# Spectral swap with real and imaginary rows on even and odd partitions; two more slices transposed by DMA

## Chip, core and metric

The kernel runs on one core of a Trainium2 chip. The core has TensorE (PE), VectorE (DVE), ScalarE (ACT), GpSimd (POOL) and SyncE (SP), each with an instruction queue of its own, and 16 DMA engines. The metric is the device time of one execution in microseconds (us); a comparison rests on the median of several executions.

## What is computed

Two kinds of layers alternate, twice each, on a sequence of 2048 positions with 512 channels (bf16):

```
def A(q, k, v, shift_k, ssm_k, ssm_D):            # long convolution
    k_shift = sum over t of k_pad[:, t:t+S] * shift_k[:, 3-t]     # 4 taps
    kv = k_shift * v
    y = irfft(rfft(kv padded to 4096) * rfft(ssm_k padded to 4096))[:S]
    return q * (y + kv * ssm_D)

def B(x, w1, b1, w2, b2):                          # MLP, 512 -> 1376 -> 512
    return gelu(layernorm(x) @ w1 + b1) @ w2 + b2

x = A_q
x = x + A(layernorm(x), ...) ; x = x + B(layernorm(x), ...)
x = x + A(layernorm(x), ...) ; x = x + B(layernorm(x), ...)
```

The part y of A depends on k, v and the filter only, so it is computed once and used in both layers.

## The kernel before

**The front: the convolution.** The Fourier transform over time is split into two stages, both matmuls against tables. The filter `ssm_k` is transposed (tag `ht`), goes through stage 1 (`h1`, L764) and stage 2 (`h2`, L777) and becomes the spectrum H, in the region `R_H`. The table S2 of stage 2 has the real part in output rows 0 to 63 and the imaginary part in rows 64 to 127. For each frequency the complex product of H with the spectrum X of kv needs H once as it is and once with real and imaginary rows exchanged. The exchanged copy lies in `R_HS`; 16 DMAs of 256 KB each make it, from partitions 0 to 63 to 64 to 127 and back:

```
for kh in range(2):
    for d0, n in PARTS:
        for c in range(0, 128 * n, 4096):
            for g in range(2):
                src, dst = [A(64 * p, 64, r + o, [512, 8], [1, 256]) for p, r in ((g, R_H), (1 - g, R_HS))]
                dma(dst, src, 1 << 18, reads=[src], rate=210.0)
```

kv is made from k and v, for two groups of 128 channels by banded matmuls on TensorE (`shift_pe`, L808, L825, product with v L832) and for the other two by VectorE (`shift_tt`, the 128x2048 forms of L656). It goes through stage 1 (`x1`, L764) and stage 2 (`products`, tags `x2_0` and `x2_64` for the two parts of 64 groups of four channels, L870). Each PSUM result is copied to SBUF by ScalarE or VectorE (`evac`, L661 or L662), and VectorE multiplies it in place with H and the exchanged copy (L656). `inverse1` (`i1_0`, `i1_64`, L894, table U) and `inverse2` (`i2_0`, `i2_64`, L951, table T2) bring y back to the time domain.

**The rest: the layers.** Sixteen slices of 128 positions are taken in blocks: `BLOCKS0` = 1, 1, 2, 2, ... in the first pair of layers, four blocks of four slices in the second. For each slice VectorE makes statistics (L983, L985), GpSimd the inverse root (L989, L991), VectorE normalizes (L998), multiplies by y and adds (L656); statistics and normalization follow again for the MLP. The normalized slice is transposed into `R_XT`: slices 0 to 3 of the first pair of layers by four TensorE transposes (L1045) and a copy out of PSUM, all others by one DMA transpose issued on SP (L1037). `m1` (L1058) multiplies by w1, ScalarE applies the gelu (L1063), `m2` (L1091) multiplies by w2, and VectorE adds the result to x (L1095). The last slice has a finer form (L1080, L1084).

**The order.** Every operation is declared to a planner (`Prog`) with an assumed duration. `Prog._cells` maps operands to cells (in four groups of 32 partitions), from which the dependencies come. `schedule` then fixes the order on each engine and, for operations that either ScalarE or VectorE can do, the engine. It uses assumed durations and tables of biases by tag (`BIAS`, `SHY`) and by operation number (`PB`, `PS`, `HOLD`, `ENG`). Each engine works through its list in order. On SP the order is: inputs, table S2, U, W1, the swaps, T2, the x input `A_q`, W2, then the DMA transposes and the stores.

Of the kernel before, what the change touches and what calls it, by code (L numbers as in the profile page):

```python
# [44 lines left out]
class Prog:  # L45
# [6 lines left out]
    BIAS = {'': -521155, 'fir0': 1051798, 'fir1': 843097, 'fir2': 989049, 'fir3': 987651, 'h1': 1081037, 'h2': -15927, 'ht': 1112634, 'i1_0': 1897872, 'i1_64':  # L52
        1957624, 'i2_0': 1184460, 'i2_64': 1481308, 'm1': 2555275, 'm2': -1895730, 'q0': 888240, 'q1': 774644, 'q19': 368770, 'q2': 596884, 'q20':
        169092, 'q21': -27345, 'q22': 917115, 'q3': 746810, 'q4': 810080, 'q5': 973212, 'q6': 1402410, 'q7': 321282, 'q8': 747916, 'taps': 871203,
        'warm0': 1001221367, 'x1_0': 904949, 'x1_1': 332081, 'x1_2': 669567, 'x1_3': 179302, 'x2_0': 377722, 'x2_64': 1746588, 'y0': 402006, 'y1':
        377011, 'y19': 351016, 'y2': 526293, 'y20': 1353266, 'y21': 1084298, 'y22': 962110, 'y3': 501697, 'y4': 829124, 'y5': 1453849, 'y6': 1171227,
        'y7': 417695, 'y8': 201523, 'z0': 1335006, 'z1': 1302874, 'z19': 54792, 'z2': 645169, 'z20': 1225188, 'z21': 742421, 'z22': -322863, 'z3':
        -681085, 'z4': 290073, 'z5': -723046, 'z6': 31881, 'z7': 125204, 'z8': 150269}
    SHY = {'fir0': 1381, 'fir1': 0, 'h1': 616, 'h2': 0, 'ht': 1476, 'i1_0': 1122, 'i1_64': 0, 'i2_0': 355, 'i2_64': 600, 'x1_0': 0, 'x1_1': 0, 'x1_2': 0,
        'x1_3': 0, 'x2_0': 175, 'x2_64': 0, 'z0': 1278, 'z1': 0, 'z2': 218}  # L60
    PB = {0: 34576, 2: -79378, 3: 43127, 4: 998812279, 9: 1394230, 44: 1395437, 45: 1613596, 47: 734111, 49: 928776, 51: 998512784, 52: 998468674, 53: -251398,
        54: -275617, 55: -73100, 56: -94401, 57: -104470, 58: -97344, 59: -11254, 60: -108406, 61: -94351, 63: -1000973, 64: -999971, 65: 27771, 66:
        -77522, 67: -999603, 68: 141227, 69: -1000923, 70: -1052691, 71: 34934, 72: -77472, 73: 998216537, 74: 133836, 75: -847532, 76: -193783, 77:
        998086816, 78: 213997, 79: -845232, 80: -158480, 81: 998714645, 82: -29228, 83: 998096074, 85: -912875, 86: 81387, 87: -823698, 88: -168262,
        89: 998118247, 90: 94211, 91: 998328931, 92: 27535, 93: -765996, 94: -165174, 95: -789736, 96: -295, 97: -846123, 99: -845182, 100: -158430,
        101: 998114703, 102: -218608, 103: 998118297, 104: -163885, 105: 998086766, 106: 912895, 107: -54439, 108: 950031, 109: -33246, 110: 1149468,
        111: -31803, 112: 1348311, 113: 217100, 114: 974687, 115: 999587069, 116: 918924, 117: 999198541, 118: 903029, 119: 999587119, 120: 909361,
        121: 217391, 122: 694743, 123: 999618935, 124: 958333, 125: 999612320, 126: 1042905, 127: 219847, 128: 900863, 129: 999657213, 130: 964412,
        131: 999608609, 132: 768388, 133: 999620187, 134: 856071, 135: 999410698, 136: 724031, 137: 999546617, 155: 23799, 156: -162015, 157: -60642,
        158: -461494, 159: -153347, 161: -694106, 162: 1454, 163: -947997, 164: 207759, 165: 998395730, 166: -173754, 167: 998555574, 169: 998332526,  # L70
        170: -423295, 171: 998606664, 172: 38904, 173: 998455595, 175: 999072054, 176: 243913, 177: 154045, 178: 391385, 179: 999289091, 180: 348447,
        181: 999128447, 183: 29584, 184: -999103, 185: 998165866, 186: 998199123, 187: 998019345, 188: 998017691, 189: 998151553, 191: -646236, 192:
        -539651, 193: 998734714, 194: -523620, 195: 998581986, 196: -137633, 197: 998715658, 199: 86734, 200: 998494190, 201: 21973, 202: -495859,
        203: 47162, 204: 48952, 205: 59976, 207: 999452991, 208: -1197, 209: 878201, 210: 929976, 211: 999077641, 212: 730704, 213: 999240348, 215:
        999293389, 216: 725624, 217: 510366, 218: 999271422, 219: 646616, 220: 381726, 221: 999070258, 222: 94055, 223: 349589, 224: 999293339, 225:
        71120, 226: -10853, 227: 772848, 228: 711543, 229: 2558, 230: 999128706, 231: 107444, 232: -203830, 233: 1276613, 234: 384777, 235: -85060,
        236: 790445, 237: 75982, 239: -823960, 240: -697909, 241: 997632090, 242: -339336, 243: -1075953, 244: -656610, 245: -826734, 246: 50, 247:
        -1076003, 248: -339386, 249: 997632040, 250: -210520, 251: -489040, 252: -675432, 253: -825900, 255: -927034, 256: -854615, 257: -1353528,
        258: 997762488, 259: -607871, 260: -1334318, 261: -871126, 262: 997876284, 263: -1321, 264: -704597, 265: 997906582, 266: 148883, 267:
        -675809, 268: -909457, 269: -70780, 270: -56569, 271: -864218, 272: -104560, 273: -36737, 274: -577323, 275: -1480713, 276: -833598, 277:  # L80
        997878740, 279: -1162936, 280: 27, 281: -687297, 282: -121406, 283: -1363624, 284: -118911, 285: 997939634, 286: 577508, 287: -393821, 288:
        475975, 289: -885280, 290: -270112, 291: 997939684, 292: 576726, 293: 998145513, 308: 1177488, 309: 1198831, 310: 1304423, 311: 1244639, 312:
        971190, 314: 285666, 315: -57020, 316: 391644, 317: -46141, 318: 998762253, 319: -155518, 320: 135422, 321: -64658, 322: 346129, 324:
        998409091, 325: -1207668, 326: 998414402, 327: -319349, 328: -1037091, 329: -441577, 330: -1032463, 331: -1024485, 332: -884533, 334: -54361,
        335: -51188, 336: -3436, 337: 322745, 339: -19921, 340: 770364, 341: 119508, 343: 150496, 344: -815052, 345: -1074024, 346: -1087676, 347:
        -942418, 348: -900262, 349: -695458, 350: 351759, 351: -892088, 352: 1076614, 353: -2671, 354: 885814, 355: -1190402, 356: 1001895, 357:
        -1433063, 358: 1027075, 359: -1429074, 360: 1029921, 361: -1731382, 362: 919746, 363: -910238, 364: 41149, 365: -890772, 366: 1184682, 367:
        -897821, 368: -1245948, 369: -144705, 370: -1245720, 371: -401600, 372: 2730439, 373: 4887400, 374: 3740474, 375: 2124032, 377: 112340, 378:
        10032, 379: -338853, 380: -245578, 382: 104508, 383: 805647, 384: -77071, 386: -911065, 387: -70724, 388: -451068, 389: -405580, 390: -950972,
        391: -206569, 392: 187780, 393: 885471, 394: -1662575, 395: 1009734, 396: -1295021, 397: 1024703, 398: -1183431, 399: 1037432, 400: -1248538,  # L90
        401: -255605, 402: -654317, 403: -359159, 405: -1278286, 407: 1092663, 408: -888363, 409: 917474, 410: 814, 411: 890156, 412: -211373, 413:
        -358377, 414: 32750, 415: 5020518, 416: 4338250, 417: 3211311, 418: 2415420, 420: -46159, 421: -2327, 422: -267214, 423: 164122, 424: 265989,
        425: -113051, 427: 110610, 428: 892080, 429: 111401, 430: -44629, 431: -261436, 432: -173254, 433: -363932, 434: 23598, 436: 42311, 437:
        12952, 438: -285134, 439: -300486, 440: 216702, 441: 228190, 442: 255444, 443: 205358, 444: 625548, 445: -22042, 446: 108479, 447: 664113,
        448: 1243693, 449: 863420, 450: -179909, 451: -322256, 452: -471129, 453: 1004937, 454: -629654, 455: 863470, 456: -761928, 457: 1009668, 458:
        -890636, 459: -156707, 460: -292462, 461: -1267645, 462: -913360, 463: -782357, 464: -540612, 465: -252368, 466: -913588, 467: -1302020, 468:
        -435191, 469: -251282, 470: -907822, 471: 3209413, 472: 3720996, 473: 4860599, 474: 3269555, 475: 3378084, 476: 4978144, 477: 4979058, 478:
        2905911, 480: -367979, 481: -368512, 482: -100350, 483: -498935, 484: 138365, 485: -92505, 487: -76592, 488: -174921, 489: 24557, 490: 185584,
# [105 lines left out]
    def _cells(self, ap):  # L204
        t = ap.tensor
# [15 lines left out]
        if t.name not in self.state:  # L221
            self.state[t.name] = np.zeros(4 * nq, dtype=np.int64)
# [345 lines left out]
AR = 105600  # L568
# [563 lines left out]
```

## Time and profile before

| | |
|---|---|
| median of 6 runs | 242.23 us (241.29 to 244.15) |
| profiled execution, its own time | 242.01 us |
| its span, first to last instruction | 240.2 us |
| PE / DVE / ACT / POOL busy | 229.7 / 179.4 / 140.0 / 33.9 us |
| granted TensorE clock | 1.000 |
| swap DMAs (`ar<-ar`) | 16 x 256 KB, median 5.9 us from issue to landing |
| DMA transposes (L1037) | 28, median 2.5 us from issue to landing |
| TensorE transposes (L1045) | 16 matmuls, in slices 0 to 3 |

Times in the profile are counted from the start of the span. A row of the chain or the timeline has a start, a length and what ran. PE is a matmul, PEld a weight load beside it, SPq the issue of a DMA on SP. A busy PE is not PE at its peak, since matmuls are pipelined and their ends are modelled. "issue" is time in which an engine waited for nothing that the profile shows.

### The profile page before, as it was taken

The numbers are of one execution on the slowest core, as the hardware profiler recorded it, in microseconds if no ns is written. First come the engines' busy times: TensorE is split into PE (matmuls) and PEld (weight loads), VectorE is DVE, ScalarE is ACT, GpSimd is POOL, SyncE is SP. The second block draws the span as 40 slices with busy tenths as digits, with TensorE's granted clock in tenths as the row PEclk, the third lists the DMA queues.
The fourth block names the chain that finished last, engine by engine and source line by source line (L and its number), as shares of the span: only waits on it lengthen the run. The fifth ranks groups of instructions, "written<-read, shape, count | busy, mean of one in ns | idle before, by whom it ended". The sixth has DMA issues, their size and how long they took to land.

```text
span 240.2 us, 5585 instructions
## 1 busy us (share of the span) xinstructions
PE 229.7 (96%) x2338; PEld 153.7 (64%) x2338; DVE 179.4 (75%) x366; ACT 140.0 (58%) x222; POOL 33.9 (14%) x75
## 2 busy tenths in 40 slices
PE   6999999877999999999999999999999999999996
PEld 2987777765889888676866774754444444444444
DVE  0689999999999899889999999999887200302223
ACT  2299999989995986553762481546412774124400
POOL 3340000000103221232131113030212000000000
PEclk9999999999999999999999999999999999999999
DMA  6999999999980000221121002406041100411103
GB/s 237 350 385 385 385 191 209 196 203 296 397 293 4 3 0 3 44 33 29 32 44 30 16 4 44 87 1 90 0 87 44 46 0 0 87 44 44 43 25 109
DMA packets 35947, 27.14 MB, mean 113 GB/s; under 512 B 18418, under 2 KB 28881, under 8 KB 35922
## 3 DMA queue, kind: packets, MB, share of 16 engines
q1 hardware_dynamic: 35358, 26.65, 41.0%
q8 instruction: 18, 0.29, 0.5%
q10 hardware_dynamic: 564, 0.14, 0.4%
q14 instruction: 7, 0.06, 0.1%
HBM read 16.82 MB, written 2.10 MB: 79 GB/s over the span
## 4 chain that ended last, share of the span: by engine, by line
PE 71%; DVE 12%; ACT 6%; DMA 4%; SPq 3%; issue 2%; DVEq 0%
PE ps L1058 32%; PE ps L1091 31%; DVE ar L656 9%; ACT ar L661 6%; DMA ar<-in_A_v_dram 4%; SPq L645 3%; PE ps L894 3%; PE ps L951 3%; DVE ar L662 2%; DVE ar L832 1%; PE ps L1080 1%; PE ps L870 1%; PE ps L1045 0%; PE ps L764 0%; PE ps L777 0%
## 5 line engine op out<-in xcount | busy, mean ns | idle before, releaser
L1063 ACT ACTIVATE ar<-ps,sm 128x256 bf16<-128x256 f32 (+4 forms) x143 | 68.2, 521 | 74.8 <-PE ps L1058 71.1
L1058 PE MATMUL ps<-ar 128*128 128x256 bf16 (+4 forms) x572 | 83.1, 297 | 0.0
L1091 PE MATMUL ps<-ar 128*128 128x512 bf16 (+1 forms) x341 | 79.9, 379 | 0.0
L661 ACT ACTIVATE ar<-ps 128x1024 bf16<-128x1024 f32 (+2 forms) x78 | 70.8, 1029 | 11.0 <-PE ps L764 5.0
L1058 PEld LDWEIGHTS ps<-ar 128*128 128x128 bf16 (+1 forms) x572 | 53.4, 100 | 28.8 <-ACT ar L1063 0.4
L656 DVE TENSOR_TENSOR ar<-ar 128x512 bf16<-128x512 bf16 (+3 forms) x108 | 64.4, 627 | 1.2 <-ACT ar L661 0.4
L1091 PEld LDWEIGHTS ps<-ar 128*128 128x128 bf16 (+1 forms) x341 | 33.1, 98 | 35.1 <-ACT ar L1063 0.4
L1095 DVE TENSOR_TENSOR ar<-ar,ps 128x512 bf16<-128x512 bf16 x31 | 20.8, 677 | 43.4 <-PE ps L1091 43.2
L983 DVE BATCH_NORM_STATS2 sm<-ar 128x6 f32<-128x512 bf16 (+1 forms) x68 | 42.7, 650 | 0.3
L998 DVE TENSOR_SCALAR ar<-ar,sm 128x512 bf16<-128x512 bf16 x64 | 23.5, 403 | 3.6 <-POOL sm L991 3.6
L991 POOL TENSOR_TENSOR sm<-sm 128x2 f32<-128x2 f32 (+2 forms) x26 | 20.2, 776 | 2.2
L764 PE MATMUL ps<-ar 128*64 128x128 bf16 x512 | 17.6, 221 | 1.5 <-ACT ar L661 0.8
L662 DVE CAST ar<-ps 128x1024 bf16<-128x1024 f32 x16 | 19.0, 1209 | 0.0
L989 POOL TENSOR_SCALAR sm<-sm 128x2 f32<-128x2 f32 (+2 forms) x26 | 5.3, 205 | 91.3 <-DVE sm L985 91.1
L764 PEld LDWEIGHTS ps<-ar 128*64 128x64 bf16 x512 | 14.9, 110 | 3.9 <-ACT ar L661 1.8
L894 PE MATMUL ps<-ar 128*128 128x128 bf16 x256 | 14.8, 219 | 0.9 <-DVE ar L656 0.9
L894 PEld LDWEIGHTS ps<-ar 128*128 128x128 bf16 x256 | 14.4, 113 | 1.2 <-DVE ar L656 1.2
L662 DVE COPY ar<-ps 128x2048 bf16<-128x2048 bf16 (+1 forms) x8 | 7.3, 918 | 8.6 <-PE ps L747 8.6
L870 PE MATMUL ps<-ar 128*128 128x64 bf16 x256 | 9.8, 193 | 3.2 <-ACT ar L661 1.7
L985 DVE BATCH_NORM_AGGREGATE sm<-sm 128x2 f32<-128x6 f32 (+1 forms) x64 | 11.1, 177 | 0.7
L870 PEld LDWEIGHTS ps<-ar 128*128 128x128 bf16 x256 | 8.3, 98 | 4.6 <-ACT ar L661 2.9
L777 PE MATMUL ps<-ar 128*128 128x128 bf16 x128 | 8.7, 220 | 0.3 <-ACT ar L661 0.2
(33 smaller groups left out, 77.4 us busy)
## 6 DMA issues: line engine op xcount, KB each, us to landing
ar<-tab_s SPq DMA_DIRECT2D x16, 256.0 KB, 9.9
ar<-ar SPq DMA_DIRECT2D x16, 256.0 KB, 5.9
ar<-in_A_ssm_k_dram SPq DMA_DIRECT2D x4, 512.0 KB, 5.4
ar<-in_A_k_dram SPq DMA_DIRECT2D x8, 256.0 KB, 7.4
ar<-in_A_v_dram SPq DMA_DIRECT2D x8, 256.0 KB, 9.9
ar<-in_A_q_dram SPq DMA_DIRECT2D x4, 512.0 KB, 7.9
out_dram<-ar SPq DMA_DIRECT2D x7, 256.0 KB, 2.0
ar<-in_B_w_dram SPq DMA_DIRECT2D x1, 1376.0 KB, 11.2
```

What stands on the lines that cost most here:

```text
L656: return P.op(eng, lambda e: e.tensor_tensor(o, a, b, op), dur, reads=[a, b] + list(more), writes=[o])
L661: return e.activation(dst, src(), AF.Copy)
L662: return e.tensor_copy(dst, src())
L764: r = e.matmul(Q(tl, 64 * ri, 64, i * 128, [1, 128]), w, m, start=True, stop=True)
L870: r = e.matmul(Q(tl, 0, 128, i * pitch, [1, n]), w, m, start=True, stop=True)
L894: r = e.matmul(Q(tl, 0, 128, i * 128, [1, 128]), w, m, start=q == 0, stop=q == 1)
L983: P.op(DVE, lambda e, sj=sj, x=x: e.bn_stats(sj, x), 40.0 + 1.1 * w, reads=[x], writes=[sj], gate=gate)
L998: P.op(DVE, lambda e: e.tensor_scalar(o, x, m, r, ALU.subtract, ALU.mult), 335.0, reads=[x, m, r], writes=[o])
L1058: r = e.matmul(Q(tl, 0, rows, 0, [1, w]), a, m, start=dk == 0, stop=dk == 3)
L1063: P.op(ACT, lambda e, dst=dst, tl=tl, rows=rows, bias=bias, w=w: e.activation(dst, Q(tl, 0, rows, 0, [1, w]), AF.Gelu_apprx_tanh, bias=bia ...
L1091: r = e.matmul(Q(tl, 0, 128, 0, [1, 512]), ins[fc][0], ins[fc][1], start=fc == 0, stop=fc == 10)
L1095: P.op(DVE, lambda e, x=x, tl=tl: e.tensor_tensor(x, x, Q(tl, 0, 128, 0, [1, 512]), ALU.add), 640.0, reads=[x], writes=[x], tile=tl)
```

## The change

Real and imaginary parts of the spectra H and X now alternate on even and odd partitions. The columns of S2 and the rows of U are permuted for it when the tables are made on the host. The 16 swaps read every second partition (step 2, from 0 or 1) and write the other 64. The planner's assumed rate for them is 370 instead of 210, and its dependency cells tell even from odd partitions. Slices 2 and 3 of the first pair of layers are transposed by DMA, as the later slices are. The planner's tables `BIAS`, `SHY`, `PB`, `PS`, `HOLD` and `ENG` have new values throughout; they are left out below.

```diff
         nq = -(-row // self.G)
-        q = np.arange(p0 // 32, (p0 + np_ - 1) // 32 + 1)
+        step = max(1, dims[0][0] // row)
+        q = np.unique((np.arange(np_) * step + p0) // 32 * 2 + (np.arange(np_) * step + p0) % 2)
...
-            self.state[t.name] = np.zeros(4 * nq, dtype=np.int64)
+            self.state[t.name] = np.zeros(8 * nq, dtype=np.int64)
...
-    S2 = S2.reshape(128, 128 * 128)
+    S2 = S2.transpose(0, 1, 2, 3, 5, 6, 4).reshape(128, 128 * 128)
...
-    U = U.reshape(128, 256)
+    U = U.transpose(1, 2, 0, 3, 4, 5, 6).reshape(128, 256)
...
+    def PA(p0, off, *dims):
+        return bass.AP(ar, p0 * AR + off, [[2 * AR, 64]] + [list(d) for d in dims])
...
-                    src, dst = [A(64 * p, 64, r + o, [512, 8], [1, 256]) for p, r in ((g, R_H), (1 - g, R_HS))]
-                    dma(dst, src, 1 << 18, reads=[src], rate=210.0)
+                    src, dst = [PA(p, r + o, [512, 8], [1, 256]) for p, r in ((g, R_H), (1 - g, R_HS))]
+                    dma(dst, src, 1 << 18, reads=[src], rate=370.0)
...
-                if L or s >= 4:
+                if L or s >= 2:
                     zs = A(0, 128, z, [1, 512])
                     P.op(SP, lambda e, zs=zs, dst=dst: e.dma_start_transpose(dst, zs), 1300.0, reads=[zs], writes=[dst],
                          dma=True, nbytes=1 << 17)
```

## The prediction

> **What bounds the kernel now.** I read the busy tenths first, then the chain of waits, then the windows of the stages, then the DMA issues. The page's tenths (40 slices of 6.0 us):
>
> ```profile
> PE   6999999877999999999999999999999999999996
> DVE  0689999999999899889999999999887200302223
> ACT  2299999989995986553762481546412774124400
> DMA  6999999999980000221121002406041100411103
> GB/s 237 350 385 385 385 191 209 196 203 296 397 293 4 3 0 3 44 33 29 32 44 30 16 4 44 87 1 90 0 87 44 46 0 0 87 44 44 43 25 109
> ```
>
> Two halves. Up to about 70 us (the convolution) VectorE, ScalarE and the DMA engines are all full and TensorE has holes. After that TensorE alone is full. In the DMA row slices 5 to 8 stand out: the engines are as busy as before, yet move about 200 GB/s instead of 385. Those are the swaps. The chain, in order of time, around the joint of the halves and around the transposes that the change moves:
>
> ```profile
> 62.93 1.22 DVE ar L662
> 64.14 5.68 DVE ar L656 x5
> 69.83 0.05 issue
> 69.87 7.34 PE ps L894 x128
> 77.21 6.55 PE ps L951 x60
> ...
> 90.08 0.45 PE ps L1058 x8
> 90.53 0.22 PE ps L1045 x4
> 90.75 0.22 PE ps L1058 x4
> 90.97 0.86 PE ps L1091 x4
> 91.84 0.22 PE ps L1058 x4
> 92.06 0.22 PE ps L1045 x4
> ```
>
> The last spectral product on VectorE (L656) ends at about 69.8 us and releases the inverse transform (L894). From 69.87 on every piece of the chain is TensorE without a gap until 237.94, where the last addition and the store follow. So the end is the end of the last product, plus 168.1 us of TensorE work, plus a fixed tail. The change can act in three ways: an earlier last product, less work in the 168.1 us, or a hole in it. The windows say how much room there is before the last product (columns: length, busy time of PE, PEld, DVE, ACT and POOL with counts, clock, DMA share, GB/s):
>
> ```profile
> 20.00:30.00 10.00, 9.60 (x152) 7.51 (x146) 10.00 (x10) 9.74 (x11) 0.00 (x0) 1.00 1.05 385
> 30.00:40.00 10.00, 9.51 (x160) 7.75 (x161) 9.97 (x9) 9.85 (x12) 0.00 (x0) 1.00 1.02 200
> 40.00:50.00 10.00, 9.27 (x247) 7.86 (x246) 9.87 (x10) 9.98 (x12) 0.38 (x2) 1.00 1.20 199
> 50.00:60.00 10.00, 6.78 (x181) 5.59 (x178) 9.48 (x9) 9.22 (x11) 0.00 (x0) 1.00 1.15 258
> 60.00:70.00 10.00, 9.01 (x177) 8.62 (x174) 10.00 (x10) 10.00 (x12) 1.04 (x2) 1.00 1.04 382
> ```
>
> In these 50 us VectorE is idle for 0.68 us and ScalarE for 1.21 us, most of both between 50 and 60. The list of waits has no VectorE, ScalarE or TensorE wait on a swap (`ar<-ar`).
>
> **The swaps (L645).** 16 transfers of 256 KB, 4.19 MB. They start at 32.8 us, and the low rate lasts until about 57, the loads queued behind them included. The first is issued in 0.72 us with the queue empty (262 KB / 0.72 us = 364 GB/s), later ones take 1.0 to 1.75 us: the queue pushes back. Count, bytes and 512-byte pieces stay the same; only the partitions change. Bounds for the new rate: 200 GB/s (nothing gained; the row of the swaps) and 385 (the loads over 128 partitions). [...] I take the upper end, since the reach is what differs between the two rows: 4.19 MB / 385 GB/s = 10.9 us instead of 21, some 10 us of DMA time.
>
> What is that worth? Little. Behind the swaps wait T2 (1 MB), X (2 MB) and W2 (1.3 MB), which land by about 72 us. T2 is first read at 76.99, X at 69.74, W2 at 86.35, and TensorE is gapless when it gets there. The products start at 49.73 and run back to back because VectorE has other work until then, and it is full. What can go is the stall at 50 to 57: a TensorE gap of 1.24 us at 50.45 that nothing in the profile releases, then ScalarE 0.78 idle and VectorE 0.39. Lower bound of the gain: VectorE's 0 (stall stays or moves). Upper: both engines' idle time of 20 to 70 us is filled, (0.68 + 1.21) / 2 = 0.95 us. I take 0.7, between the 0.52 us that VectorE lost in the 50-to-60 window and the 0.95. What is late next is VectorE's own 1.2 us per product (16 of them) and 1.2 us per PSUM copy, which the change leaves.
>
> **Layout (the tables S2 and U).** Their columns and rows are permuted on the host: same bytes, same matmuls of L777, L870 and L894. H, its swapped copy and the product X all take the same partition order, so no instruction is added: 0. The finer dependency cells (two parities in each of four groups of 32) keep the two directions of a swap apart as the halves did: 0.
>
> **The tables of the planner.** Priorities, holds and engine choices are all new, so the order on every engine may change, though every operation of the front remains. By itself this can be worth either sign; the rivals take it up.
>
> **Slices 2 and 3 transposed by DMA.** Removed: two groups of 4 TensorE transposes (L1045), 0.22 us each on the chain = 0.44 us, and two copies out of PSUM, of which ScalarE did one (0.59) and VectorE one (0.41). Added on SP: two DMA transposes. SP has nothing else then: its loads are issued by 58.6 and its next instruction is at 97.05, so no queue is held up. Their cost from the 28 that are there:
>
> ```profile
> L1037 SPq DMA_TRANSPOSE ar<-ar x28: 1189/1264/1407, 97.0 to 207.2; - x28
> DMA to landing us min/median/max: 2.4/2.5/4.2
> ```
>
> Slice 3's normalization (L998) ends at about 90.75; issued at 90.85, it lands at 93.35, and with the wake-up the first m1 matmul of this block (L1058) can start at about 93.5. Now it starts at 93.16; without the transposes TensorE would reach it at 92.7. So 0.8 us need cover. There is some: of the 22 m2 matmuls (L1091) of slices 0 and 1 only 15 are done by then, and the 7 left are 7 x 0.216 = 1.5 us. Covered, the sum is -0.44; without cover +0.35 (-0.44 + 0.8). [...] The row here shows 2.5 us for the whole slice, issue included. I go by the row: -0.44. VectorE's 0.41 us is worth nothing on the chain, as TensorE has no hole there.
>
> **Sum.** -0.44 - 0.7 = -1.14 us. On the profiled execution (242.01 us, span 240.2) that is 240.9. The median shown is 242.23, so for the median 241.1.
>
> **Rivals.**
> [...]
> 2. *The new order shortens the front by more.* ScalarE is idle 2.53 us before 77.25. Its copies of the first inverse half, done before 70 though TensorE needs them only at 77, could go there; in their place ScalarE takes two 1.13 us copies from VectorE before the last product: 2.3 us more, 242.23 - 1.14 - 2.3 = 238.8. For it: all tables are new, and earlier landings of swaps and T2 leave the order freer. Against: nothing waited on the swaps.
> 3. *Slower: work pushed behind the last product.* Between 70 and 84.7 VectorE is busy 13.99 of 14.7 us and must deliver the normalized slices 0 and 1, which TensorE takes at 83.5, with its own work running out at 84.4. Spare there: 0.7 us. If the new order defers three VectorE copies (3.4 us), TensorE stands 3.4 - 0.7 = 2.7 us, and the time is 242.23 - 1.14 + 2.7 = 243.8. It decides from 0.7 + 1.14, some 1.8 us, of deferred VectorE work. Against: ScalarE has 2.9 us to spare there.
> [...]
>
> **How the numbers follow.** Forecast 0.48 (241.1, own range 239.9 to 242.4), rival 1 0.10, rival 2 0.21, rival 3 0.16, rival 4 0.05. A measurement of this kernel tells about 1% (2.4 us) from no change: bounds 239.8 and 244.65. Faster: 0.19 of rival 2 and 0.05 of the forecast's lower end = 0.24. Slower: rival 4 and half of rival 3 = 0.13. Within: 0.63. The range 238.2 to 244.8 leaves out 0.06 below (rival 2 at its best) and 0.12 above.
>
> **What would show it.** Right: the swaps' windows show well over 200 GB/s with the issue nearer 0.7 us; VectorE and ScalarE stay full from 20 us to the last product, which ends at 68.5 to 69.5; L1037 counts 30 and L1045 8; the chain is gapless TensorE after it, 167.6 us long. Wrong: a last product before 67.5 (rival 2), a TensorE gap between 70 and 95 (rival 3 or the transposes), VectorE waiting on `ar<-ar` (rival 4), swaps still near 200 GB/s (rival 1).

## The result, and the profile after

The changed kernel takes 241.77 us (median of 34 executions; all but one between 241.28 and 242.74), the kernel before 242.54 us in the same comparison (71 executions). The ratio is 0.9964, with a 95% interval of 0.995 to 0.9978: 0.9 us less, or 0.8 by the two medians. (The ratio leaves out executions disturbed on the chip.) The prediction had said 241.1 us. The two profiled executions cannot show this by their length: before 242.01 us, after 242.08 us, both with a span of 240.2 us. The first lies half a microsecond below its median, the second 0.3 above. So I read the traces for their parts, and leave the total to the medians.

The page's tenths after the change (40 slices of 6.0 us):

```profile
DVE  0499999999997988989999996978897401211214
ACT  2589899999998994665556243464532552436200
DMA  6999989799930002222020203313022203210022
GB/s 233 347 387 385 385 197 286 209 276 319 384 118 3 3 0 48 45 44 48 0 44 3 44 1 69 65 23 68 0 43 44 87 3 67 64 44 3 0 98 76
```

In slices 5 to 8 (30 to 54 us, counting from 0) the DMA row is no longer 9 throughout, and more moves. The rate is not 385, though. The windows of the stages (us, busy time of PE, PEld, DVE, ACT and POOL with counts, clock, DMA share, GB/s):

```profile
30.00:40.00 10.00, 9.23 (x169) 7.92 (x167) 9.80 (x9) 10.00 (x12) 0.00 (x0) 1.00 0.91 233
40.00:50.00 10.00, 9.30 (x236) 7.72 (x234) 9.83 (x10) 9.72 (x11) 0.38 (x2) 1.00 0.89 240
50.00:60.00 10.00, 7.34 (x194) 6.05 (x191) 9.97 (x10) 9.87 (x12) 0.49 (x1) 1.00 0.96 299
60.00:70.00 10.00, 9.30 (x176) 8.81 (x177) 10.00 (x10) 10.00 (x12) 0.55 (x2) 1.00 0.85 304
```

From 50 to 60 VectorE is now busy for 9.97 us (9.48 before) and ScalarE for 9.87 (9.22). The swaps' issues on SP take 780 ns in the middle (594 to 1161; before 1090, 649 to 1640), and they land in 3.5 us instead of 5.9. The DMA transposes:

```profile
L1039 SPq DMA_TRANSPOSE ar<-ar x30: 1189/1264/1627, 89.5 to 202.9; - x30
DMA to landing us min/median/max: 2.4/2.5/2.7
```

The chain of waits around the joint (line numbers have moved by 2: L896 is the inverse transform, L953 its second stage, L1047 the TensorE transposes, L1060 and L1093 the two matmul groups of the MLP):

```profile
65.23 3.83 PE ps L896 x64
69.06 0.10 issue
69.16 8.20 PE ps L896 x144
77.36 0.45 PE ps L953 x4
...
83.15 0.34 DVE ar L1000
83.48 0.05 issue
83.53 0.40 PE ps L1047 x4
...
91.91 3.03 PE ps L1093 x14
94.93 3.93 PE ps L1060 x36
```

The inverse transform resumes after the last product at 69.16 instead of 69.87, that is 0.71 us earlier. But the chain goes on to the same last addition at 237.98 (before 237.94). Between lie 168.8 us instead of 168.1. Three terms make up the 0.75 us of difference. The new order leaves 144 matmuls of L896 behind this point instead of 128 (8.20 - 7.34 = +0.86). Two groups of transposes are gone (-0.44). And TensorE waits 0.33 us at 83.5 for VectorE's normalization (L1000), which the page's waits list as one wait of L1047. In these two executions, then, what came in at the front went out again behind it. (The change at the front is not all due to the swaps: the new order also moves one of VectorE's PSUM copies, 1.2 us, from between the products to behind them.) Where the measured 0.9 us come from had to be found by taking the change apart.

### The profile page after: what moved, and what is told of

Its sections match the earlier page's. It is cut to its first block, busy times and chain, and to the rows that moved or that the text cites. A ratio compares the mean times of both kernels' runs of the same rounds, so it can differ in the third digit from the quotient of the medians.

```text
span 240.2 us, 5579 instructions
## 1 busy us (share of the span) xinstructions
PE 229.4 (95%) x2330; PEld 153.4 (64%) x2330; DVE 175.5 (73%) x363; ACT 142.6 (59%) x223; POOL 34.7 (14%) x75
## 4 chain that ended last, share of the span: by engine, by line
PE 79%; DVE 11%; ACT 6%; DMA 1%; issue 1%; ACTq 0%
PE ps L1060 32%; PE ps L1093 31%; ACT ar L663 6%; DVE ar L658 6%; PE ps L896 5%; DVE ar L664 4%; PE ps L766 3%; PE ps L749 2%; PE ps L827 1%; DMA ar<-in_A_shift_k_dram 1%; PE ps L1082 1%; DVE ar L834 1%; PE ps L810 1%; PE ps L872 1%; DVE sm L985 1%
## 5 line engine op out<-in xcount | busy, mean ns | idle before, releaser
L1065 ACT ACTIVATE ar<-ps,sm 128x256 bf16<-128x256 f32 (+5 forms) x143 | 67.7, 521 | 72.9 <-PE ps L1060 70.1
L1060 PE MATMUL ps<-ar 128*128 128x256 bf16 (+5 forms) x572 | 84.0, 297 | 0.0
L1093 PE MATMUL ps<-ar 128*128 128x512 bf16 (+1 forms) x341 | 81.1, 379 | 0.0
L663 ACT ACTIVATE ar<-ps 128x1024 bf16<-128x1024 f32 (+2 forms) x79 | 73.7, 1068 | 8.6 <-PE ps L749 2.5
L1060 PEld LDWEIGHTS ps<-ar 128*128 128x128 bf16 (+1 forms) x572 | 53.2, 100 | 29.3 <-ACT ar L1065 0.4
L658 DVE TENSOR_TENSOR ar<-ar 128x512 bf16<-128x512 bf16 (+3 forms) x108 | 63.7, 628 | 0.3
L1093 PEld LDWEIGHTS ps<-ar 128*128 128x128 bf16 (+1 forms) x341 | 33.1, 98 | 34.6
L1000 DVE TENSOR_SCALAR ar<-ar,sm 128x512 bf16<-128x512 bf16 x64 | 24.1, 401 | 6.3 <-POOL sm L993 6.3
L991 POOL TENSOR_SCALAR sm<-sm 128x2 f32<-128x2 f32 (+2 forms) x26 | 5.8, 224 | 95.9 <-DVE sm L987 95.8
L664 DVE CAST ar<-ps 128x1024 bf16<-128x1024 f32 (+1 forms) x15 | 17.6, 1181 | 0.7 <-PE ps L766 0.2
L896 PE MATMUL ps<-ar 128*128 128x128 bf16 x256 | 15.1, 220 | 1.0 <-DVE ar L658 0.5
L896 PEld LDWEIGHTS ps<-ar 128*128 128x128 bf16 x256 | 14.5, 114 | 1.4 <-ACT ar L663 0.8
L664 DVE COPY ar<-ps 128x2048 bf16<-128x2048 bf16 (+1 forms) x6 | 5.7, 956 | 9.4 <-PE ps L749 9.2
```

The lines of the kernel that those rows point to most:

```text
L658: return P.op(eng, lambda e: e.tensor_tensor(o, a, b, op), dur, reads=[a, b] + list(more), writes=[o])
L663: return e.activation(dst, src(), AF.Copy)
L664: return e.tensor_copy(dst, src())
L896: r = e.matmul(Q(tl, 0, 128, i * 128, [1, 128]), w, m, start=q == 0, stop=q == 1)
L1000: P.op(DVE, lambda e: e.tensor_scalar(o, x, m, r, ALU.subtract, ALU.mult), 335.0, reads=[x, m, r], writes=[o])
L1060: r = e.matmul(Q(tl, 0, rows, 0, [1, w]), a, m, start=dk == 0, stop=dk == 3)
```

## Experiments

**The two halves of the change, each alone.** Runs e1 and e2 put interleaving with the old order against the new order without interleaving.

```diff
e1: before.py, all of it but the following kept (same order on every engine)
+    S2 and U permuted, the dependency cells by parity
-    src, dst = [A(64 * p, 64, r + o, [512, 8], [1, 256]) for p, r in ((g, R_H), (1 - g, R_HS))]
+    src, dst = [PA(p, r + o, [512, 8], [1, 256]) for p, r in ((g, R_H), (1 - g, R_HS))]
e2: the changed kernel, with the same lines turned back (same order as the changed kernel)
```

Expected of e1: 

> The kernel before, with only the swaps and the two tables S2 and U interleaved; the order on every engine is that of before. Theory A (the faster swaps take the stall at 50 to 57 us away): -0.4 to -0.9 us against before, swaps near 286 GB/s, last product before 69.3 us. Theory B (nothing waited on the swaps; the gain comes from the transposes and from the new order): within 0.2 us of before, although the swaps run at 286 GB/s too.

Expected of e2: 

> The changed kernel with the swaps and tables put back on halves; its order, engine choices and DMA transposes stay. Theory A: it loses the front's share, 0.4 to 0.9 us slower than the changed kernel, swaps near 200 GB/s. Theory B: as fast as the changed kernel within 0.2 us, that is 0.6 to 1.0 us faster than before. If the new order leans on the faster swaps, a VectorE wait on a swap shows near 51 us and it is slower than before.

Measured, against 242.74 in this comparison: e1 241.84 (ratio 0.9964, 0.9937 to 0.999), e2 242.14 (0.9971, 0.9945 to 0.9996). The interleaved swaps alone, with not one instruction moved, give as much as the whole change. The new order and the DMA transposes without them give some 0.6 us, and the two gains do not add up. The intervals of e1 and e2 overlap, so nothing more is read from their difference.

What the interleaving does is seen where TensorE runs dry, near 51 us. The timeline of TensorE, first in the kernel before:

```profile
47.99 2.46 PE L870 MATMUL ps<-ar 128*128 128x64 bf16 x66
51.68 1.51 PE L870 MATMUL ps<-ar 128*128 128x64 bf16 x46 [1.24 <-issue]
```

and in e1 (L870 is L874 there):

```profile
48.35 3.33 PE L874 MATMUL ps<-ar 128*128 128x64 bf16 x96
51.93 0.64 PE L874 MATMUL ps<-ar 128*128 128x64 bf16 x16 [0.26 <-ACT ar L665]
```

The 1.24 us before the matmul at 51.68 end with nothing that the profile shows ("issue"). In e1 the same matmuls run without it, until they wait for a PSUM copy of ScalarE, which is the limit there anyway. From 46 to 58 us VectorE goes from 11.38 to 11.90 us of 12 and ScalarE from 11.22 to 12.00. The inverse transform resumes at 69.53 instead of 69.87. VectorE's products at that place, in the kernel before, in e1 and in e2:

```profile
49.73 5.99 DVE L656 TENSOR_TENSOR ar<-ar 128x2048 bf16<-128x2048 bf16 x5
56.10 6.90 DVE L656 TENSOR_TENSOR ar<-ar 128x2048 bf16<-128x2048 bf16 x6 [0.39 <-ACT ar L661]
...
50.08 12.58 DVE L660 TENSOR_TENSOR ar<-ar 128x2048 bf16<-128x2048 bf16 x11
...
51.38 18.25 DVE L658 TENSOR_TENSOR ar<-ar 128x2048 bf16<-128x2048 bf16 x16
```

This shows why the two gains do not add up. In e2 TensorE has its gap too (1.03 us at 52.06), but in the new order the 16 products run through it in 18.25 us, as long as in the changed kernel (18.26). The faster swaps and the new order remove the same stall of VectorE.

**Further traces of the kernel before** (e9, e10, e11: the kernel before, unchanged). Its times had shown a second group near 243.2 to 245 us, and a profile of such an execution was wanted.

Expected of e9: 

> The kernel before, for further traces: its times spread from 241.3 to 245.4 us and gather near 242 and near 244, those of the changed kernel stay below 242.8. Theory A2 (the stall at 50 us is at times long enough to lower TensorE's clock): a trace of 243 us or more shows a gap of over 1.5 us near 51 and a granted clock below 1 in the 6 us behind it, with the last product 1 to 2 us later than 69.8. Theory D (the late k load at 16 us does it): it shows a gap of 2 us or more at 14 to 17 us and a clock of 0.5 behind it, and the same delay. A trace near 242 us shows neither.

Expected of e10: 

> A further trace of the kernel before: as for the look before it. Theory A2: 243 us or more goes with a long gap near 51 us. Theory D: with a long gap at 14 to 17 us.

Expected of e11: 

> A third further trace of the kernel before: as for the two before it. Theory A2: 243 us or more goes with a long gap near 51 us. Theory D: with a long gap at 14 to 17 us.

Measured 242.49, 242.34 and 242.56: none fell into the upper group. But all three show the "issue" gap at the same matmul, of 1.17, 0.93 and 1.48 us. Over all traces it is in every one with swaps between halves (before 1.24; 0.69 to 1.48 in the others with the old order, and 1.03 in e2). With interleaved swaps it is absent in e1 and both profiles of the changed kernel, and short in e6 and e4 (0.37 and 0.63 us). Gaps of this kind are not gone altogether: the changed kernel's profile has two, of 0.58 and 0.72 us, at 17 and 24 us, where the loads fill the DMA engines (the DMA row at 9, 385 to 387 GB/s). They lie far ahead of the products.

These traces also give the gain without the medians. With the old order and the full clock (before, e9, e10, e11, e1, e12) 170.3 to 170.4 us pass from the moment when the inverse transform resumes to the end of the span. The time is therefore decided by that moment: 69.87, 70.36, 70.09 and 70.43 with the swaps between halves, 69.53 in e1 and 69.75 in e12, on average 0.55 us earlier. The 16 products with the copy among them take 19.8 to 20.3 us in the first four and 19.4 in the last two. When they begin varies from trace to trace (49.7 to 50.3) with either kind of swap. e7, again with swaps between halves, fits with its short gap of 0.69 us: its products take 19.55 us, and as they begin early, at 49.65, the transform resumes at 69.25.

**What ends the gap.** The profile names no releaser, but the packets in the traces show one. The page's table of DMA queues has a queue for instructions:

```profile
q8 instruction: 18, 0.29, 0.5%
```

These are 18 packets of 16 KB, and one comes for every 256 TensorE instructions (18 x 256 = 4608, of 4676 matmuls and weight loads on the page), so they are read here as TensorE's program, 16 KB / 256 = 64 bytes an instruction by that reading. Over the 13 traces of the full computation TensorE has 22 "issue" gaps of more than 0.17 us after the first 10 us. All 22 stand at the same place of the count, 189 to 194 instructions behind a multiple of 256 (a few records are missing), and all end 1.3 to 1.6 us after such a packet has ended.

The packet ahead of the gap near 51 us, first in the kernel before (48.5 to 50.5 us), then in e1 (46.5 to 48.5 us):

```profile
q8 instruction: 1, 0.02, 4.1%
q8 instruction: 1, 0.02, 3.3%
```

The shares are of 16 engines in 2 us, thus 1.32 and 1.04 us. In the kernel before, the 256 instructions ahead of the gap start at 46.12 and are through at 50.45. The packet with the next ones starts only 2.62 us after 46.12 and takes 1.32, and TensorE goes on 1.62 later: 5.56 us in all, 1.2 more than the 4.33 that TensorE had work for. In e1 it starts 0.76 us after the same point and takes 1.04, and TensorE comes to its instructions 2.9 us after it has ended. I take it that TensorE waited for its own program, whose packet came late among those of the swaps (DMA share 1.15 from 46.12 to 50.45). This is read from the traces; no run changes the instruction packets alone.

**Swaps with an eighth of the bytes** (e12): would swaps that cost nothing give more than e1?

```diff
-                    dma(dst, src, 1 << 18, reads=[src], rate=210.0)
+                    o8 = dma(dst, src, 1 << 18, reads=[src], rate=210.0)     # order planned as before
+                    o8.fn = the same swap with [512, 1], [1, 256] instead of [512, 8], [1, 256]
+    8 memsets of R_HS on GpSimd, ahead of the swaps
```

Expected of e12: 

> The kernel before in its old order, with each swap cut to an eighth of its bytes (64 x 256 elements of 64 x 8 x 256; the rest of the exchanged copy is zeros, written by GpSimd between 15 and 32 us, so the spectral products are wrong in value and the same in time). It leaves out 7/8 of the swaps' traffic and shows what the swaps cost at all. Theory A (the full DMA engines cause the stall at 50 us): no gap that nothing releases near 51 us, and 0.9 us less than before, as with interleaved swaps; then faster swaps have nothing more to give. If the swaps cost more than that, it is faster than the kernel before with interleaved swaps (241.8). If the stall has another cause: the gap of about 1.2 us is there, and the time is that of before.

Measured 241.72 us against 242.69 (0.9957, 0.9927 to 0.9986), without the gap at 51 us; DMA engines busy for 0.24 of the time from 40 to 50 us. That is what e1 gives, within the intervals. So faster swaps have about 1.0 us to give in all, and interleaving takes practically all of it.

**What the swaps' rate depends on** (e8: no computation; six batches of 16 SBUF-to-SBUF transfers of 256 KB, one after the other). The batches: halves of the partitions in pieces of 512 bytes (the old swap), halves with 4 KB, even to odd partitions with 512 bytes (the new swap), even to odd with 4 KB, all 128 partitions with 512 bytes, all 128 with 2 KB.

Expected of e8: 

> Leaves out the whole computation. It moves 4.19 MB from SBUF to SBUF six times, each time 16 transfers of 256 KB followed by a wait: between halves in 512-byte pieces (as before) and in 4 KB rows; between even and odd partitions in 512-byte pieces (as after) and in 4 KB rows; over all 128 partitions in 512-byte pieces and in 2 KB rows. [...] If the pieces set it (or their issue, 0.86 us for 256 KB): even/odd in 4 KB rows rises to about 385, and whole in 512-byte pieces is near 286.

The windows of the six batches (us, GpSimd's busy time, clock, DMA share, GB/s):

```profile
14.00:34.00 20.00, 0.00 (x0) 1.00 1.08 210
36.00:53.00 17.00, 0.00 (x0) 1.00 1.03 240
56.00:70.00 14.00, 0.00 (x0) 1.00 1.02 287
72.00:81.00 9.00, 0.00 (x0) 1.00 1.01 404
84.00:98.00 14.00, 0.00 (x0) 1.00 1.01 287
101.00:111.00 10.00, 0.00 (x0) 1.00 1.02 381
```

Two limits, one behind the other. Half of the partitions gives 210 GB/s with 512 bytes and 240 with 4 KB. Every second partition of all 128 goes as high as all 128 do (287 and 287 with 512 bytes, 404 with 4 KB and 381 with 2 KB), so the alternation costs nothing here. What holds the new swap at 287 are its 512-byte pieces, by the 404 of the 4 KB ones. It is not the issue on SP, since the engines are full in all six batches (share 1.01 to 1.08). In the changed kernel itself the rate was 286 GB/s from 44 to 50 us; over 30 to 50 us it was lower on average (233 and 240), at a DMA share of 0.91 and 0.89, so the engines were not full throughout.

**The DMA transposes without the new tables.** First two kernels in which the planner orders anew, with the old tables: e3 with the old swaps, e4 with the interleaved ones.

```diff
-                if L or s >= 4:
+                if L or s >= 2:          # e3; e4 with the lines of e1 as well
                     P.op(SP, ... e.dma_start_transpose(dst, zs) ...)
     the numbered tables stay attached to the same operations as before
```

Expected of e3: 

> The kernel before, with only slices 2 and 3 transposed by DMA; the order of the front is that of before, the planner orders what follows the first slices anew. The sum of the prediction: -0.44 us (eight TensorE transposes less), no TensorE gap between 84 and 96. If the cover by m2 of slices 0 and 1 is missing: +0.35 us, with a TensorE gap of some 0.8 us near 93.

Expected of e4: 

> The kernel before with both edits, interleaved swaps and DMA transposes of slices 2 and 3, and with the old planner tables. Theory A with the transposes: -0.87 to -1.3 us against before, at least as fast as the changed kernel. Theory B with the transposes: -0.44 us. What is missing to the changed kernel's -0.87 us is then the share of the new tables.

Measured: e3 248.34 us (1.0245, 1.0191 to 1.0298), e4 247.54 (1.0191, 1.0153 to 1.023). Both are about 5 us slower. The trace of e3 shows where: TensorE waits for DMA transposes (1.8 us in two waits, the longer 1.07 us at 94.5) and for VectorE's additions to x (L1102, four waits, 2.7 us). The old tables, tuned for another set of operations, give a bad order here. So e3 and e4 tell what the tables are worth, and not what two DMA transposes cost. For that, e6 and e7 replace the transposes in the finished order and leave every other instruction in its place.

```diff
e6: e1, and after planning, for s in (2, 3):
-   the four TensorE transposes (PE) and their copy out of PSUM
+   q = P.order[SP]; q.insert(<by start time>, dma_start_transpose(dst, zs))    # L1125
    what waited for the copy waits for the DMA
e7: the same with the swaps between halves
```

Expected of e6: 

> The kernel before with interleaved swaps, and slices 2 and 3 transposed by DMA with every other instruction kept in its old order on its engine (so m2 of slices 0 and 1 is not moved in front of m1 of slices 2 and 3). The prediction's sum without cover: +0.35 us against the kernel before with interleaved swaps (-0.9 against before), so -0.5 against before, with one TensorE gap of about 0.8 us, released by the DMA, near 92.5. If the DMA lands in time: -1.3 us against before.

Expected of e7: 

> The same fixed order and DMA transposes, with the swaps on halves as before: +0.35 us against before without cover, -0.44 with it. Its front is that of before, so its trace is a second look at that front: theory A expects a TensorE gap that nothing releases (0.6 to 1.5 us) between 50 and 53 here again, and none in the run with interleaved swaps and the same order.

Measured, against 243.34 in this comparison: e6 246.06 (1.0085, 1.0051 to 1.012), e7 247.44 (1.0161, 1.0107 to 1.0214). The chain of e6 around the transposes of slices 2 and 3, and their landing (one line from the source line's view):

```profile
90.14 1.05 DVE ar L1002 x3
91.19 0.03 DVE ar L660
91.21 4.03 DMA ar<-ar
95.25 0.05 issue
```

```profile
DMA to landing us min/median/max: 2.5/3.3/4.0
```

TensorE stands 2.74 us, until 95.29. The normalization that comes last is the third of three in a row and ends at about 91.2 (by the order of the program it is slice 2's; slice 3's ended 2.3 us before), and its transpose lands 4.03 us after the issue begins. That is +2.74 - 0.44 = +2.3 us by the trace, and 244.33 us for that execution against 241.66 for the profiled one of e1.

Why 4.03 and not 2.5? Not because it follows another transpose: the changed kernel issues the same two closer together (1.43 us apart instead of 2.24), and they land in 2.54 and 2.46 us. The table of queues for 91.25 to 95.2 us in e6 has one packet more:

```profile
q8 instruction: 1, 0.02, 1.4%
ar<-ar SPq DMA_TRANSPOSE x1, 4.0
```

It is a 16 KB packet of TensorE's program, from 93.19 to 94.07. All of the transpose's packets but two have run by 93.25, and the last two, of 4 bytes, run at 94.05 and 94.06. Over the 13 traces of the full computation 28 of 378 transposes took over 2.65 us, and each of the 28 has an instruction packet within its time (so have some of the others). In the changed kernel the next such packet starts at 93.60, 0.23 us after the landing.

The changed kernel is spared for a second reason. Its new order normalizes slice 2 before slices 4 and 5, so that the second transpose is issued at 90.91, and puts 14 matmuls of L1093 at that place (3.03 us at 91.91), so that TensorE does not wait. It runs in 241.91 us in this comparison (e5, the changed kernel again: 0.9941, 0.9911 to 0.9972).

Expected of e5: 

> The changed kernel once more, beside the next two on one chip, for a second trace of it. Theory C (the gain is the faster swaps alone; the transposes and the new order add nothing net): about -0.9 us against before, as the kernel before with interleaved swaps alone showed (-0.9). Theory of the prediction (swaps 0.7, transposes 0.44): 0.4 us better than that kernel, -1.3.

By its ratio e5 lies 1.4 us below the kernel before, which looks like the -1.3 of the prediction's theory. It does not decide for it: in this comparison 14 of 23 executions of the kernel before lost clock, as the next part shows, and at full clock the difference is 0.63 us.

**The second group of times is a drop of the granted clock.** e6's twelve times fall into two groups: four between 244.15 and 244.52, eight between 245.47 and 247.32. The mean clock that each execution was granted tells them apart: 1.000 in all of the four, 0.993 or 0.986 in all of the eight. e7's profile caught such an execution (0.993 in the mean, 245.51 us). Its windows around the gap of 2.67 us before the first m1 matmul at 94.88:

```profile
94.00:96.00 2.00, 1.12 (x6) 0.82 (x7) 1.97 (x7) 0.05 (x1) 0.89 (x2) 0.70 0.00 0
96.00:98.00 2.00, 2.00 (x11) 1.44 (x10) 1.14 (x5) 1.76 (x5) 0.95 (x2) 0.50 0.33 65
98.00:100.00 2.00, 2.00 (x22) 1.78 (x20) 1.60 (x4) 0.82 (x4) 0.00 (x0) 0.95 0.01 0
```

The clock (the column after POOL) is halved once TensorE starts again, and recovers 3.4 us later. From 96 to 98 only 11 matmuls run, from 98 to 100 there are 22. The three rows lose 0.3 x 2 + 0.5 x 2 + 0.05 x 2 = 1.7 us of full clock, which is 0.7% of the span: one such drop makes a mean of 0.993, and two would make 0.986 (an estimate from this one; no trace has that mean). The drop followed a gap of 2.1 us (e4, clock 0.50 from 18 to 20) and one of 2.7 us (e7), and in e6's profile it did not follow one of 2.74 us (clock 1.00 throughout).

The same reading of the timed executions:

| kernel | clock 1.000 or 0.999 | clock 0.993 or 0.986 |
|---|---|---|
| before (in the comparisons of e1/e2, e5/e6, e12) | 34, median 242.39 us | 29, median 243.81 us |
| changed kernel, both times | all | none |
| e1 and e12 | 21, 241.31 to 242.76 us | 3, 241.97 to 242.19 us |
| e2 | 11 | 1 (242.42 us) |
| e6 | 4, 244.15 to 244.52 us | 8, 245.47 to 247.32 us |
| e7 | none | 6, 245.51 to 248.46 us |
| e3 | 4, 247.58 to 248.44 us | 2, 250.20 and 250.84 us |
| e4 | 5, 247.42 to 247.63 us | 1 (247.81 us) |

What a drop costs depends on where it falls. In e4's trace it lasts from 18 to 21.4 us, in the front, where VectorE is the full engine (2.00 us of each 2), and that execution is some 0.3 us longer than the other five; the three of e1 also lie only some 0.3 us up. In e6, where TensorE is the limit behind the gap, the upper group lies 1.8 us up.

So the gain has two parts. At full clock it is some 0.5 to 0.6 us over all: 242.39 against 241.77 to 241.91. (By comparison it is 0.66 in e1's, 0.63 in e5's and 0.09 in e12's, so this figure is no sharper than that.) The rest is that nearly half of the executions of before lose clock, once or twice by that estimate, which costs 1.4 us by the medians, and those of the changed kernel don't. The table also says what is not gained: the shortest executions, 241.21 us both before and after, are alike.

## Why the prediction was right, and where it was not

- **The stall, -0.7 us: right.** The place (50 to 57 us), the direction and the size hold: e1 gives -0.9 us, of which about 0.7 at full clock. What the prediction could not name is the reason of the stall, by the traces the late instruction packet. In the changed kernel VectorE's 16 products run back to back from 50.76, and the last one ends at 69.0, inside the predicted 68.5 to 69.5; there the new order would have removed the stall by itself (e2).
- **The rate, 385 GB/s: too high.** It was 286. The prediction went by the loads over 128 partitions, with the reach as the only difference; that was an estimate which no run had shown, and it left out the pieces. In e8 the reach does tell (210 against 287 GB/s), and the 512 bytes tell as well (287 against 404). The estimate did no harm, since e12 with an eighth of the bytes is no better than e1.
- **The transposes, -0.44 us: the saving is there, the working of the cover was wrong.** In the changed kernel no wait for a transpose is left, and both land in 2.5 us, as taken. But in the old order, for which the cover was worked out, 2.7 us (e6) were needed instead of 0.8. Two terms were wrong. The normalization was put at 90.75, where the first of three in a row ends. Both slices are needed, and the last of the three ends at 91.2 in e6 and, in the trace of before too, they run from 90.40 for 1.06 us. And the median landing of 2.5 us was taken for the one transfer that TensorE waits for. That was 4.0 us in e6 and e7, where an instruction packet crossed it (in e6 from 93.19 to 94.07), near the 4.2 that the row of before shows as its maximum. Without cover the edit costs +2.3 us in this order, not +0.35. With the 1.5 us of cover that was counted, 2.74 - 1.5 = 1.2 us would have stayed open, a net of +0.8 us; with a landing in 2.5 us those 1.5 us would have been enough (2.74 - 1.53 = 1.2). The row was the right one to go by, since 2.5 us for a whole slice is what most transposes take (at most 2.65 in 350 of 378), but with its upper end as a risk.
- **No gap in the chain, 167.6 us of TensorE: the step that failed.** It is 168.8. The prediction put the new order at nothing in its sum and left it to the rivals. The new order does bring the cover, 14 matmuls, and it pays for it elsewhere: 0.86 us of inverse transform behind the last product and 0.33 us of waiting at 83.5. This is more than the 0.44 saved. The transposes and the new order together are worth about nothing on top of the interleaving: 241.77 and 241.91 against e1's 241.84.
- **The sum, -1.14 us, measured -0.9**, agrees in size, then, in part by luck. One term of two holds, the other was eaten up by the new order, and some of the 0.9 us is clock drops that disappeared, which the prediction did not have.
- **The rivals.** Rival 1 (the swaps gain no speed) falls by 199 to 286 GB/s. Rival 4 (slower swaps) falls by the same 286, and by e8 with its 404 GB/s between even and odd partitions. Rival 2 (a front shortened by more) does not happen: the last product ends 0.8 us earlier, not 3. Rival 3 (work behind the last product, a wait for the normalized slices) names the right place, 83.5 us, but it is 0.33 us and not 2.7.
- **A small misreading:** the later swap issues took 0.65 to 1.64 us, not 1.0 to 1.75. Nothing hangs on it.

**What stays open.** That the gap near 51 us comes from the swaps is shown: in the old order it is gone when they alone are made faster or smaller (e1, e12), and short in e6 (0.37 us). That it is a wait for instructions is read from where the packets stand in the traces, without a run that moves them alone. A clock drop of the kernel before itself was not caught in a profile, so its place there is open. The gap near 51 us, in a stretch where TensorE is only two thirds busy, is a candidate, since e1 and e12 differ from before in it and have no execution in the upper group. Against it, e2 has the gap as well (1.03 us), and one drop in twelve. A second candidate (theory D in what was expected of e9) is the wait for a load of k near 15 us, which lasts 1.86 us in e10, 1.92 in e12 and 2.11 in e4, where the drop follows it. Against this one, that drop cost little, and e1 and e12 have the same order there.

## What to carry to other kernels

A DMA that nobody waits for can still cost time while it keeps the engines full (0.9 to 1.0 us here, e1 and e12, at a DMA share of 1.02 to 1.20 in the kernel before): look for "issue" gaps of a busy engine inside a stretch of low GB/s at a full DMA share, and then for the packets of the instruction queue in front of them. When a DMA takes over work from an engine, size the cover by the slowest landing that its row shows as well as by the median (4.2 and 2.5 us here), since each of the 28 of 378 here that took over 2.65 us had an instruction packet within its time; and expect an order tuned around the old instruction to need tuning again (+5 us here with the old tables, +2.3 us with the old order). Where a kernel's times fall into two groups, read each execution's mean clock first: 0.7% of 240 us is one drop to half for some 3.4 us, and in two traces here (e4, e7) it follows a TensorE gap of 2.1 or 2.7 us, while in e6 none follows one of 2.74 us.

## What the hardware showed that was not expected

- Between partitions of SBUF, over all 128 or from even to odd, pieces of 512 bytes hold the DMA engines to 287 GB/s, where 2 to 4 KB reach 381 to 404 (e8).
- Alternate partitions reach as much as all 128 (e8): 404 GB/s with 4 KB against 381 with 2 KB, and 287 each with 512 bytes, while one half gives 240 with 4 KB and 210 with 512 bytes.
- The trace counts 18 instruction packets of 16 KB on the same 16 DMA engines, one for every 256 TensorE instructions. TensorE's 22 "issue" gaps of 0.2 to 1.5 us (13 traces) all end 1.3 to 1.6 us after such a packet, and the one near 51 us in the kernel before stands where the packet started only 2.62 us after the 256 instructions ahead of the gap (0.76 in e1), at a DMA share of 1.15.
- A 128x512 DMA transpose landed in at most 2.65 us in 350 of 378 cases. The other 28, up to 4.5 us, each had an instruction packet within their time, as had some of the 350.
- After a TensorE gap of 2.1 or 2.7 us the clock was halved for 3.4 us (e4, e7), but not after one of 2.74 us in the profiled execution of e6, nor after 1.86 and 1.92 us (e10, e12).
